# A searched order replaced by another: attention and MoE on one core, with each load tied to an exponential of its own

## The chip, the core and the metric

The kernel runs on one core of a Trainium2 chip. The metric is the device time of one execution in microseconds; the median of three runs of the kernel before is 357.67 us (357.56 to 357.82).

## What is computed

Attention with pooled queries for 8 batches of 8 heads, and a two-branch maximum layer on its output:

```python
B, H, S, D = 8, 8, 1152, 64
q_pool = q.reshape(B, H, S // 2, 2, D).mean(axis=3)          # 576 queries a head
scores = (1.0 / sqrt(D)) * q_pool @ k^T                       # 576 x 1152
attn = softmax(scores);  attn_out = attn @ v                  # 576 x 64
x = attn_out.transpose(0, 2, 1, 3).reshape(B * 576, 512)      # 4608 tokens
h1 = x @ w1;  h2 = x @ w2                                     # 512 x 1024 each
out = maximum(h1, h2) @ w_out                                 # 1024 x 512
```

Inputs and output are float32; the kernel's matmuls take bfloat16.

## The kernel before

The kernel writes every engine's instruction list out of one recorded order. `Plan.op` records an operation with its engine, what it reads and what it writes; `Plan.solve` works out which semaphores each must wait for, and leaves out waits that are already known to be over; `emit` then writes each engine's operations in the recorded order. No engine looks ahead: PE (TensorE), ACT (ScalarE), DVE (VectorE), POOL (GpSimd) and SP, which issues nearly all DMAs, each go through their own list in turn.

The order itself is one long string. Each letter is one step: `S` a group of scores, `E` an exponential, `A` one chunk of attention times V, digits `0` to `3` one unit of a MoE job (each digit is a stream with a job of its own), `l` the next load on SP, `k`, `q`, `v` POOL's casts of K, Q and V, `t` the DMA that transposes K, `x` the DMA that transposes the attention output, `r` one of eight DVE transposes of pooled Q, `e` POOL's copy of a remainder, `o` a store, `4` to `9` copies out of PSUM. Which load is next stands in `LOADS`, which MoE job is next in `MOE` (`w`: product of the weights, `h`: the difference branch, `p`: the output projection), and which PSUM bank a score group or a job takes in `BANKS`.

- **Attention.** Two heads make a head pair; there are 32. K, Q and V of a pair are loaded in float32 (576 KB each) into one of three buffers, and cast by POOL to bfloat16 (`cast_k`, L405; `cast_q`, which also adds neighbouring queries, L435; `cast_v`, L445). K is transposed by a DMA on SP (`ktrans`, L475), Q by DVE (`qtrans_dve`, L485); the first pairs go through PE (L533, L552).
- **Scores and exponentials.** The pairs' scores form one row of 324 groups of 512 columns for both heads; `scores` (L302) fills two PSUM banks with a group, `exps` (L317) has ACT write its exponential to `et`. Where a group crosses into the other half of `et`, ACT does it in two pieces, so there are 336 instructions.
- **Attention times V** (`av_jobs`, L621; remainders L636): nine matmuls make a chunk of 128 queries of one head. V carries a column of ones, which gives the sums; DVE takes reciprocals (L651) and scales (L654).
- **MoE.** maximum(h1, h2) = h2 + relu(h1 − h2), so the kernel keeps `wd` = w1 − w2 (L506) and `w21` = w2·w_out (L593). `h_jobs` (L760) computes relu(x·wd), copied out by DVE or ACT (L771, L775); `p_job` (L803) adds x·w21 and relu·w_out over 24 matmul units per 256 tokens, copied out at L809 or L812 and stored (L829, L835). The last tokens go as `z` jobs (L846).

Scores, MoE matmuls and transposes use half of the PE array's rows at a time in pairs ("64*128" in the profile); attention times V uses all rows ("128*128").

A load waits for its buffer and, from the 40th exponential on, for the exponential two before the one that stands last in the recorded order at the load's place:

```python
def pace():
    g = done[0] - PACE
    return [f"E{g}"] if PACE and g >= PACE_FROM else []
```

Of the kernel before, what the change touches and what calls it, by code (L numbers as in the profile page):

```python
# [116 lines left out]
def bass_funnel_attn__then__act_maxout2_kernel(  # L117
# [78 lines left out]
    with ctx:  # L196
# [762 lines left out]
        for c in (  # L959
            "luFFlulllfyKQklgfbSkKEFlgFKSgESyFFlKEFgQSbESlFkSFEFFKlEySFSgESlqFFEFQlSbEFkSQElbKvSEgSlESceAAEATcESA"  # L960
            "EAhlkSaSEaASclEKAEglSAEcSAElvSaTaEhElTcSAESlAhAEScAElSSAcEAAlAqESa0a00aE0la0ScAE0SldQEaa00bSd0lEXSj0"
            "00ESvTl0h0E00eS4SlEAAkAEAlSa1ad1E1S1SEl1q1S1E1Kl1g1qE1S1SE1lQkrAEbArSdtAErArSE11avlEa1S5AElSdArESSrA"
            "dArEArSAEkAlaAaSEaAdatAESaXadjXEjSjSEXq0jl00jE0S0qr0E0lSr01rE11e41Sl1E1Sk1r10Er005St0ESv00r0ESSr0rvE"
            "lA4AAEASqalSaEAArAErAlSrSEEaAeaAArxAErSSaAEaAklrAAErS1at1ak1E1r0Sr0xE0r0Sr11E1rS1r0E050Sl0E0q0SrS0tE"
            "r01r10Er0eS0r0E0r0Skr0lE0r1S0r0E0rlSv0r1E14S11El1S1oSE1oAAEASAkEAaAlaSAEtAvSa1aE1SxS11ES111E1111ES11"
            "l1ESq5AAEAlSrSoEAroArAESrkSArEAaAalAEAaAaSvaaEtaSSrXEqArAjAEAjSrle00Ea0aS0rSE0lr0vSr0E1r01rlE114S11E"
            "1S1rSEA5AlvAEASr0E0ta0Eva0SrSE00xe00SE4AAkAESSlAEAaAaAEAlSa1aE1Sx000E0Sk11E0lS11E11S50qlE00tS00ESer0"
            "0rSE00rS0rE00r00Er0l0qSrSE0r01l1r0E14S11E1l1SroSE1r1o11roSErAoArAtEkArAAaaAArq1ESaa1E1Sx001r001E1r0S"
            "1rE0l001rS141E1rS1r1ES5AAEvAAroSSrvoESAlAAEvAaAaAlEAaAkaSa000SaEt0a000011114Ee111S111115E1S111Xl5EvS"
            "j00j0ESl0qSE0000SEl4AAAEArSSaEAaArAlqEArS1a1taE11rSESrE1e1xrS1r1EA5AAEASla0kaE0Sr00rSEq0l0r0SEr0ArAl"  # L970
            "E4SAAESr11aE1a1Srx1ESr11r1SEt5qAAAEArSe0aE0a0Slr0SEkr0S0r0E0lrS0r0E0r0Sl0rE0000ES0S0Er0tArAEArArS0aE"
            "0aq0Srx10Er1S14k1E1S11EroS1rSo1E1oAAoEvAAS1vElSAAlEAvAaSa1ESalAaAAEASa1aE1taS1rXvE1rS1j11Ej1eSrl11rE"
            "11qrSS5EAlAAkEAroS0a0oEa0S0rS0ErAAlAEASa0a0E0l0S4x00E0qSE0r00E0trSA4eAEAArS1a1Ea1k1Sr11ESr1lSr1E5AAA"
            "lEArS1a1Ea11Srx00E10S1l1E1S500tE0Sq0rS0Er00r0e0ESr00rSEl0kr00r0E0rS0l0ES00SE0A4AAEAAaAoaAoASaoSqaE11"
            "x11SESkr11t1rE11rE11rE1SrS1E1r11r1SEr11S1E1S11E1A5AEvAASoSvESlAAoAEvAaAaAElAaAa0Sa0a0E0taS00r0000E04"
            "e0Sx000r0E11141vS1x1E11r100500Sr11qE1Sr01lr110E1rS050E0Sl0r0E0SS0l0E0S0r0EArAArEAArlAkaAaArSE0etEa0a"
            "S0r0SE0rxS0rq0EA4AAEASkao1aE11o1SSE11lS11EA5AAElASa1aE1Sx0r00E0rS1rt0E0er0Sr0E1S4111ESl1r0q0E500S0lE"
            "0SrS0r0EA4lAAEAAAaaAASa1aESlk1Sx1r1ES1r11Ert11r11Er1qSSr1E1rArAEvAS1E11klS11El11vS1E1S1lvA5ESAAEAoAa"
            "oSaSESaAtaArAEArq00Ea0aSa00rExSv0r00ErS0xe0r0E0rSSr0kl0E0S00E0Sl00E0S00El0A4AEAAAaoSaSEoArAtArE00Ea0"
            "0aeS00rxE1111r00qS411E1111151S1k1E1r1Sl00500ESr000SrEl0A4AAEArSla1aE1S1S1EAAAEAlSa1aE1tSrS1rq1E1r1x1"  # L980
            "1rESSre11Er11rSk1Elr11S1E11Sl1E1A5AAEASaoSaEAoAAoEAoSa0a0tEq00rSESr0E00rx00k040E0AArvAArSrSvElArArAE"
            "AvaAaAAaAaSaSaE00a001x14E11S11E1x11Sv511E100S1SE0r1t11r0ES0500E0eSr00Er00SrSE0r00r0SEr0S00E0S00E0004"
            "0E00S0E0oS00oSE4AAAEAAaAaAeAAaEAaAAxAaAaAASa0aES0x00SE1000E0S411E1S11E111500S0E00S11E1S11E1S10E50S00"
            "E0S10E0Se10E00S00E0S00E0S00E10S41E11S11EoS11o1E1oSSo1E1AAEAAAaAaAAAaAaAxAAAAAaAaAAaAa1a1a1a11X1j11j1"
            "11111900001111111150000111o080110091o110000008101110191101000018111009101110000080101111191100000001"
            "001111910000000011111111110001000800110000o008001o11o00010181111Z9ZZZZZoZZoZZZZZZmZZZZzzZZZZZZZZZZmZ"
            "ZZZZZZzZzmzz"
        ):
            step(c)
# [52 lines left out]
```

## Time and profile before

| | |
|---|---|
| median of 3 runs | 357.67 us (357.56 to 357.82) |
| span of the profiled execution (no other time of it is given) | 356.4 us |
| PE matmul busy | 346.0 us (97%) |
| PE weight loads busy | 218.5 us (61%) |
| ACT busy | 313.8 us (88%) |
| DVE busy | 230.1 us (65%) |
| POOL busy | 151.4 us (42%) |
| exponentials (L317) | 336 instructions, 302.4 us |
| DMA | 84.55 MB, mean 237 GB/s |
| granted PE clock | 0.999 |

The span runs from the first to the last instruction of one execution. "PE" is matmuls, "PEld" the weight loads, which overlap them; the ends of matmuls are modelled, so a busy PE is not PE at its peak. In rows of waits, the engine and line on the left stood still until the one behind the arrow was done; "issue" means that the profile shows nothing that it waited for.

### The profile page before, as it was taken

What the parts mean: (1) busy time and instruction counts of PE and PEld (TensorE: products, weight loads), DVE (VectorE), ACT (ScalarE), POOL (GpSimd) and SP (SyncE); (2) the same over time, 40 slices, a digit from 0 to 9 for tenths busy, and PEclk for the clock granted to TensorE, in tenths of its full rate; (3) what the DMA queues carried; (4) which work ended last, traced back from release to release, by engine and by line L of the source; (5) the groups of instructions that cost most, each with busy time, mean ns of one, the idle gap of its engine ahead of it and who ended that gap; (6) DMA issues with size and microseconds to landing.
All of it is one profiled execution on the core that took longest, in us unless ns stands there. A gap on an engine that the chain in (4) does not pass through costs nothing.

```text
span 356.4 us, 13757 instructions
## 1 busy us (share of the span) xinstructions
PE 346.0 (97%) x6178; PEld 218.5 (61%) x6178; DVE 230.1 (65%) x472; ACT 313.8 (88%) x354; POOL 151.4 (42%) x136
## 2 busy tenths in 40 slices
PE   7889999999899999999999999999999999999996
PEld 5556665656564675656666576556576757448753
DVE  2587589974966867985887677785586875414001
ACT  5999999999999899999999989989999796992431
POOL 2625997554564264355544455227444621010000
PEclk9999999999999999999999999999999999999999
DMA  8999999999989989998999699998999943012215
GB/s 271 403 397 398 370 255 309 280 289 261 293 252 279 315 196 350 237 301 183 278 320 260 153 230 301 237 314 234 224 299 255 267 68 75 17 32 47 61 31 148
DMA packets 76699, 84.55 MB, mean 237 GB/s; under 512 B 48480, under 2 KB 49760, under 8 KB 76640
## 3 DMA queue, kind: packets, MB, share of 16 engines
q1 hardware_dynamic: 75856, 83.15, 87.5%
q8 instruction: 48, 0.79, 0.9%
q10 hardware_dynamic: 784, 0.52, 0.5%
q14 instruction: 11, 0.09, 0.1%
HBM read 62.91 MB, written 9.44 MB: 203 GB/s over the span
## 4 chain that ended last, share of the span: by engine, by line
PE 87%; ACT 9%; DMA 2%; issue 1%; SPq 0%; DVE 0%
PE ps L803 25%; PE ps L621 20%; PE ps L302 19%; PE ps L760 16%; ACT et L317 9%; PE ps L636 3%; PE ps L593 2%; DMA qraw<-in_q_dram 2%; PE ps L846 1%; PE ps L552 0%; PE ps L533 0%; SPq L346 0%; DVE qp L428 0%; SPq L358 0%; PE ps L730 0%
## 5 line engine op out<-in xcount | busy, mean ns | idle before, releaser
L317 ACT ACTIVATE et<-ps 128x1024 bf16<-128x1024 f32 (+1 forms) x336 | 302.4, 1019 | 14.5 <-PE ps L302 9.7
L302 PE MATMUL ps<-qpT,kT 64*128 64x256 bf16 (+7 forms) x1162 | 117.3, 283 | 2.7 <-issue 1.1
L485 DVE STREAM_TRANSPOSE qpT<-qp 32x288 bf16<-32x288 bf16 x216 | 101.4, 469 | 10.4 <-PE ps L302 6.1
L760 PE MATMUL ps<-xT,wd 64*128 64x512 bf16 (+3 forms) x832 | 81.2, 311 | 0.2
L302 PEld LDWEIGHTS ps<-qpT,kT 64*128 64x128 bf16 x1162 | 48.3, 94 | 49.7 <-ACT et L317 11.3
L803 PE MATMUL ps<-wo,stage 64*128 64x512 bf16 x544 | 76.4, 376 | 0.0
L435 POOL TENSOR_TENSOR qp<-qraw 128x576 bf16<-128x576 f32 x30 | 42.1, 1406 | 61.1 <-DMA qraw<-in_q_dram 57.3
L621 PEld LDWEIGHTS ps<-vE,et 128*128 128x128 bf16 x1728 | 54.9, 97 | 13.9 <-ACT et L317 9.3
L621 PE MATMUL ps<-vE,et 128*128 128x65 bf16 x1728 | 60.7, 193 | 0.7 <-issue 0.3
L771 DVE TENSOR_SCALAR stage<-ps 128x1024 bf16<-128x1024 f32 (+3 forms) x41 | 39.7, 970 | 21.1 <-PE ps L760 20.6
L760 PEld LDWEIGHTS ps<-xT,wd 64*128 64x128 bf16 x832 | 35.6, 94 | 22.2 <-PE ps L760 1.9
L405 POOL TENSOR_SCALAR kbf<-kraw 128x1152 bf16<-128x1152 f32 x31 | 35.7, 1153 | 26.3 <-DMA kraw<-in_k_dram 25.6
L803 PE MATMUL ps<-w,xT 64*128 64x512 bf16 x272 | 40.8, 377 | 0.0
L803 PEld LDWEIGHTS ps<-wo,stage 64*128 64x128 bf16 x544 | 26.4, 94 | 20.5
L445 POOL TENSOR_SCALAR vE<-vraw 128x1152 bf16<-128x1152 f32 x24 | 27.4, 1154 | 19.4 <-PE ps L636 10.8
L809 DVE COPY stage<-ps 128x1024 f32<-128x1024 f32 x14 | 17.1, 1224 | 23.1 <-PE ps L803 23.0
L468 POOL TENSOR_SCALAR stage<-et 128x1152 bf16<-128x1152 bf16 x14 | 16.1, 1152 | 35.5 <-ACT et L317 35.5
L654 DVE TENSOR_TENSOR xnat<-ps,rc 128x256 bf16<-128x256 f32 (+2 forms) x71 | 27.6, 397 | 2.0
L651 DVE RECIPROCAL rc<-ps 128x4 f32<-128x4 f32 (+2 forms) x64 | 11.6, 182 | 25.9 <-PE ps L621 25.5
L621 PEld LDWEIGHTS ps<-stage,et 128*128 128x128 bf16 x576 | 18.1, 97 | 2.7 <-issue 2.6
L621 PE MATMUL ps<-stage,et 128*128 128x65 bf16 x576 | 19.7, 193 | 0.0
L803 PEld LDWEIGHTS ps<-w,xT 64*128 64x128 bf16 x272 | 12.5, 94 | 8.8 <-DVE stage L771 0.2
(55 smaller groups left out, 155.4 us busy)
## 6 DMA issues: line engine op xcount, KB each, us to landing
vraw<-in_v_dram SPq DMA_DIRECT2D x32, 576.0 KB, 6.1
kraw<-in_k_dram SPq DMA_DIRECT2D x31, 576.0 KB, 6.7
qraw<-in_q_dram SPq DMA_DIRECT2D x31, 576.0 KB, 6.3
out_dram<-stage SPq DMA_DIRECT2D x24, 256.0 KB, 4.1
out_dram<-stage SPq DMA_DIRECT2D x21, 128.0 KB, 3.4
xT<-in_moe_w_dram SPq DMA_DIRECT2D x4, 512.0 KB, 12.2
stage<-in_moe_w_out_dram SPq DMA_DIRECT2D x4, 512.0 KB, 14.1
stage<-in_moe_w_dram SPq DMA_DIRECT2D x4, 512.0 KB, 13.2
```

Of the source, the lines that this page charges most:

```text
L302: last = e.matmul(ps[:, h, col:col + hi - lo], kT[i % 3][rows(h), t, :], qpT[i % 3][rows(h), lo:hi], start=True, stop=True)
L317: op("ACT", lambda e: e.activation(et2[:, :, c:c + z - a], ps[:, :, a - g * W:z - g * W], EXP, scale=scale), r=[f"b{m}", f"b{m + 1}"], w=w ...
L405: op("POOL", lambda g: g.tensor_scalar(kbf[s][:, :, :, :].rearrange("p t h d -> p h t d"), kraw[r][:, :, :, :], 1.0, 1.0, ALU.mult, ALU.mu ...
L435: op("POOL", lambda g: g.tensor_tensor(qpf[s][:, :, :], qraw[r][:, :, 0, :], qraw[r][:, :, 1, :], ALU.add), r=[f"qraw{r}"], w=[f"qp{s}.0", ...
L445: return g.tensor_scalar(vE[r][:, :, :, 0:D].rearrange("p t h d -> p h t d"), vraw[s][:, :, :, :], 1.0, 1.0, ALU.mult, ALU.mult)
L485: op("DVE", lambda e: e.transpose(view[dst:dst + 32, :, 32 * pb:32 * pb + 32], qpf[s][src:src + 32, :, 32 * db:32 * db + 32]), r=[f"qp{s}. ...
L621: last = e.matmul(fb[m][:, at * 66:at * 66 + 65], et[:, a:a + P], vE[vs][:, t, half, 0:65], start=(t == 0), stop=(t == NT - 1))
L654: todo.append(evac_op("DVE", lambda e, m, z=z, at=at, num=num, dst=dst: e.tensor_tensor(dst, a(m)[z, at:at + num, 0:D], rc[k][z, at:at + n ...
L760: last = e.matmul(fb[m + k][:, 0:size], wd[z, ct, (f0 + k) * P:(f0 + k + 1) * P], xT[z, ct, n0:n1], start=(turn == 0 and ct == 0), stop=(t ...
L771: return e.tensor_scalar_max(gT[:, f0:f0 + 2, g0:g0 + size], wide[m // 2][:, :, 0:size], 0.0)
L803: last = e.matmul(fb[m + k][:, :], lhs, rhs, start=(turn == 0 and j == 0), stop=(turn == 1 and j == NC_ + NF - 1))
L809: return e.tensor_copy(osb2[:, o:o + 2, :], wide[m // 2][:, :, :])
```

## The change

The order is replaced as a whole: the step string, `BANKS`, the order of `LOADS`, and one place in `MOE` are new tables. ACT copies 11 MoE results and a `z` block out of PSUM where it copied 14 and one; DVE does the others. The MoE tail uses up to four streams where it used two. The rule for loads is replaced too: a table `PACES` gives each load on SP the number of the exponential that it waits for, or −1 for none.

```diff
-    PACE = 2
-    PACE_FROM = 40
...
+    PACES = (
+        -1, -1, -1, -1, -1, -1, -1, -1, -1, -1, -1, -1, -1, -1, -1, -1, -1, -1, -1, -1, -1, -1, -1, -1,
+        -1, -1, -1, -1, -1, -1, -1, 20, -1, 22, 21, -1, 9, -1, -1, 45, 34, 41, -1, -1, 29, 50, 36, 71,
...
     MOE = (
-        "wwhhhhpphhhhpphhhhhhhhpphhhhpphhhhphhhhpphhhhphhhhphhhhpphhhhhhhhhphphh"
+        "wwhhhhpphhhhpphhhhhhhhpphhhhpphhhhphhhhpphhhhphhhhphhhhpphhhhhhhphhhphh"
...
-        def pace():
-            g = done[0] - PACE
-            return [f"E{g}"] if PACE and g >= PACE_FROM else []
-
-        done = [0]
+        def pace(eng="SP"):
+            g = PACES[issued[0] - 1] if eng == "SP" else -1
+            return [f"E{g}"] if g >= 0 else []
+
...
-                after=([f"kraw0.{c}" for c in K0] if s == 0 and hi - lo == NT else []) + pace() + old,
+                after=([f"kraw0.{c}" for c in K0] if s == 0 and hi - lo == NT else []) + pace(eng) + old,
...
-                done[0] = g
```

Of the orders, three places follow. Line numbers are those of each program; from L302 on, a line of the program before stands six or seven higher in the new one (L302 is now L309, L475 is L481, L621 is L627, L760 is L766, L803 is L809).

PE around the first run of 72 attention matmuls (L621, both heads of one pair), before:

```order
L803 MATMUL ps<-wo,stage 128x512 x8
L302 MATMUL ps<-qpT,kT 128x256 x4
L621 MATMUL ps<-vE,et 128x65 x72
L803 MATMUL ps<-wo,stage 128x512 x2
L302 MATMUL ps<-qpT,kT 128x320 x2
L302 MATMUL ps<-qpT,kT 128x192 x2
```

and now:

```order
L809 MATMUL ps<-wo,stage 128x512 x4
L309 MATMUL ps<-qpT,kT 128x256 x4
L809 MATMUL ps<-wo,stage 128x512 x6
L627 MATMUL ps<-vE,et 128x65 x72
L309 MATMUL ps<-qpT,kT 128x320 x2
L309 MATMUL ps<-qpT,kT 128x192 x2
```

Between the same two groups of scores (L302, L309) stand two units more of the output projection (two matmuls each), and they stand ahead of the run.

PE around the longest run, late in the program, before:

```order
L760 MATMUL ps<-xT,wd 128x512 x4
L302 MATMUL ps<-qpT,kT 128x384 x2
L302 MATMUL ps<-qpT,kT 128x128 x2
L621 MATMUL ps<-vE,et 128x65 x144
L302 MATMUL ps<-qpT,kT 128x448 x2
L302 MATMUL ps<-qpT,kT 128x64 x2
L760 MATMUL ps<-xT,wd 128x512 x2
```

and now:

```order
L309 MATMUL ps<-qpT,kT 128x384 x2
L309 MATMUL ps<-qpT,kT 128x128 x2
L766 MATMUL ps<-xT,wd 128x512 x2
L309 MATMUL ps<-qpT,kT 128x448 x2
L309 MATMUL ps<-qpT,kT 128x64 x2
L627 MATMUL ps<-vE,et 128x65 x45
L309 MATMUL ps<-qpT,kT 128x512 x2
L627 MATMUL ps<-vE,et 128x65 x99
L766 MATMUL ps<-xT,wd 128x512 x4
```

Two groups of scores have moved ahead: one in front of the run, and one into it.

SP around the DMAs that transpose K of head pairs 5 and 6 (kT2 from kbf1, kT0 from kbf0; `qraw`, `kraw`, `vraw` are the loads' buffers, and the semaphores are those of the engines waited for), before:

```order
L475 DMA_TRANSPOSE kT2<-kbf1 128x9x128 [waits sem_POOL]
L358 DMA qraw0<-in_q_dram 128x1152
L358 DMA qraw1<-in_q_dram 128x1152 [waits sem_ACT]
L346 DMA kraw1<-in_k_dram 128x2x576 [waits sem_ACT]
L475 DMA_TRANSPOSE kT0<-kbf0 128x9x128 [waits sem_POOL]
```

and now:

```order
L481 DMA_TRANSPOSE kT2<-kbf1 128x9x128 [waits sem_POOL]
L376 DMA vraw2<-in_v_dram 128x2x576
L376 DMA vraw0<-in_v_dram 128x2x576
L376 DMA vraw1<-in_v_dram 128x2x576
L364 DMA qraw1<-in_q_dram 128x1152
L352 DMA kraw2<-in_k_dram 128x2x576
L481 DMA_TRANSPOSE kT0<-kbf0 128x9x128 [waits sem_PE,sem_POOL]
```

Five loads, none with a wait written at it, now stand between the two; before there were three, two of which wait for ACT.

More of the change, by code (lines that the diff above doesn't have):

```diff
@@ L362, in load_q @@
                 w=([f"qraw0.{lo}"] if hi - lo < QU else [f"qraw{s}"]) + name,
-                after=(["qraw0.0", "qraw0.4"] if s == 0 and hi - lo == QU else []) + pace() + old,
+                after=(["qraw0.0", "qraw0.4"] if s == 0 and hi - lo == QU else []) + pace(eng) + old,
                 dma=f"d_qp{lo}" if hi - lo < QU else f"d_q{s}",
@@ L965, in bass_funnel_attn__then__act_maxout2_kernel @@
[L965 to L974, printed above, removed]
@@ new lines, in bass_funnel_attn__then__act_maxout2_kernel @@
+            "AElSdrSlErlXAjdAEAjSaSaEAdaAaAAEXaqSaEjXSj00Ekj0rS0SrE0kt0rS0Er01v411lE1Sl1e1lrE1Slr00vlE0r0tSr10Eq5"
+            "000SSE4AklAAEASvaSaEArAAlrEArSSEreAEArAAaEqaSSaxAaEAAAEt0aSa00rE0SrSxk0Er011r0qE0r1Sr1E141Sl11El1SrS"
+            "1Er11r00E0reS1r1E1rSq1r1E10rS1rk1ESr11r1E1vS500E00S0roESAlAAElAAaSaSErAArqAE0laSa00rxES0rS0Er00l0r0o"
+            "E0r0St0SE000SE4AAAESrSAEAAvAElSaSatAEvaAAaAEAvSaSaEaSrXEjAeAjAEAkSa0a0ESrSk0tr0ESr000qE1l0141oE1So11"
+            "E1lSSl1EA5AAEASa0at0E0Er0SrSE00rx00rSEA4AlAEAlkSrSEArAerAEAaaS0a0Ea00xSSE0000SE40k000E0SrSt0Er0S0r0E"
@@ new lines, in bass_funnel_attn__then__act_maxout2_kernel @@
+            "0re00rSE0r0q000ESS00vEr0Sr00E0q101E41S11E11roSSrE1l1Sr1t1Er1AAEAAoAaAaoAAoSEa1a1lE1r000x0S0000E14S1r"
+            "lAESrlv11r1ESr11l1E1lS5AEAASoSESAoAAElAaAaAEAaAqaSa000a0Ea0000S40k000E1S0001110Evt14111S5XEjS0j0l0Er"
+            "0lSr00Er0S0vSE4AAAeEArSSrEAAaAaqEA0aSa0E0r0klSr0El0ErSx0e0SE4AAlAEAlSat0aE0Sr00rSESr000rE0rAAE4ASAES"
+            "a0a00Er0kSr00ErS0qt0SE4AAAEeAlSa0aE00rS0r0ESr000rE0Sr00Erq0Sr00E0rSSr0E0rS0r0EArArAEAqSa0a0ESr01rk1E"
+            "lSr100Ev14S11E11SroSEArxAvrAEArSlAEAlAAlaSalSEaAxAaAEASta1a1Ea1Sr1SE1oX11joE1eSj1orSE1rl1v1rSl1E1lr1"
```

47 lines of the change are left out of this document (24 added, 23 removed), and 29 rows, old and new, of tables (LOADS, PACES).

## The prediction

> **What bounds the kernel now.** I read the page first, then the busy time by stretches, the waits, the chain, and the timeline at the places where an engine stood still.
>
> ```profile
> span 356.4 us, 13757 instructions
> PE 346.0 (97%) x6178; PEld 218.5 (61%) x6178; DVE 230.1 (65%) x472; ACT 313.8 (88%) x354; POOL 151.4 (42%) x136
> PE 87%; ACT 9%; DMA 2%; issue 1%; SPq 0%; DVE 0%
> 0.00:60.00 60.00, 54.30 (x1032) 33.70 (x1032) 40.14 (x76) 55.10 (x63) 37.88 (x42) 1.00 1.02 345
> 60.00:128.00 68.00, 66.74 (x1200) 41.88 (x1202) 51.78 (x109) 66.15 (x75) 32.93 (x28) 1.00 1.05 278
> 128.00:188.00 60.00, 59.73 (x1110) 38.33 (x1108) 45.58 (x100) 59.44 (x66) 30.62 (x27) 1.00 1.09 271
> 188.00:321.00 133.00, 132.99 (x2293) 82.36 (x2288) 87.27 (x174) 122.80 (x138) 50.00 (x42) 1.00 0.82 197
> 321.00:354.00 33.00, 32.23 (x557) 22.22 (x553) 5.30 (x16) 10.34 (x17) 0.00 (x0) 1.00 0.28 67
> ```
>
> The columns of the stretches are the busy time of PE, PEld, DVE, ACT and POOL, the PE clock, the DMA share and GB/s. Two engines are close to full. Up to 188 us ACT is the fuller one or level with PE (55.10 of 60, 66.15 of 68, 59.44 of 60), so the exponentials set the pace there. From 188 to 321 us PE is busy for 132.99 of 133 us, and ACT stands for 10.2. Behind the last exponential comes a tail of matmuls, 33 us with PE all but full. A new order that does the same work can only win where one of the two stood still.
>
> ```profile
> 9.43 15.70 ACT et L317 x17
> ...
> ACT et L317 <- PE ps L302: 9.7, 15, 2.1
> PEld ps L302 <- ACT et L317: 11.3, 48, 0.5
> PEld ps L621 <- ACT et L317: 9.3, 27, 0.6
> ...
> ACT et L317 <- PE ps L621: 2.9, 3, 1.1
> ```
>
> An exponential in the full stretch takes 15.70/17 = 0.923 us. By the wait rows (total, times, longest) ACT stood 9.7 + 2.9 = 12.6 us for PE. That is all that a better feeding of ACT could give, and most of it lies where PE was busy all the while, so it can't come back whole. PE's waits for ACT are many and short: 11.3/48 = 0.24 us each.
>
> **The change part by part.** The computation is the same, and so, nearly, is how much of it stands ahead of a given exponential. Adding up the order with unit times as the chain has them (an estimate), 46, 78, 111 and 164 us of matmuls stand ahead of exponentials 60, 96, 132 and 192 in both, and 294 and 296 ahead of the last. So the sum is one of stalls, in six terms.
>
> *1. The hole in the issue of instructions.*
>
> ```profile
> 92.70 0.61 PE L302 MATMUL ps<-qpT,kT 64*128 64x128 bf16 x8 [1.12 <-issue]
> 92.70 0.33 PEld L302 LDWEIGHTS ps<-qpT,kT 64*128 64x128 bf16 x7 [1.38 <-issue]
> ...
> 93.13 4.81 ACT L317 ACTIVATE et<-ps 128x1024 bf16<-128x1024 f32 x5 [0.49 <-PE ps L302]
> ...
> q8 instruction: 48, 0.79, 0.9%
> ```
>
> At 92.70 us PE had waited 1.12 us for nothing that the profile shows, and ACT 0.49 us behind it. The row of the instruction queue (48 packets, 0.79 MB) makes a late block of instructions the likeliest cause. Bounds: −1.1 if the hole goes or falls where ACT has scores in stock, 0 if it only moves, +1.1 if there are two. I take −1.1, since one hole in 356 us is rare and most places have cover. The Trainium skill, "Runtime: NRT & Kernel Launch", section "Instruction fetch mechanics", says that crossing a 16 KiB block is mostly hidden. The trace agrees for all but this one place; going by that rule alone, this term is 0 and the sum 1.1 us higher.
>
> *2. Long runs of attention-times-V matmuls.*
>
> ```profile
> 119.36 2.35 PE L621 MATMUL ps<-vE,et 128*128 128x65 bf16 x72
> ...
> 121.75 2.48 ACT L317 ACTIVATE et<-ps 128x512 bf16<-128x512 f32 x3 [1.15 <-PE ps L621]
> ...
> 298.02 4.52 PE L621 MATMUL ps<-vE,et 128*128 128x65 bf16 x144
> 300.40 0.38 ACT L317 ACTIVATE et<-ps 128x256 bf16<-128x256 f32 x1 [0.91 <-PE ps L621]
> 302.91 1.94 ACT L317 ACTIVATE et<-ps 128x1024 bf16<-128x1024 f32 x2 [2.12 <-PE ps L302]
> ```
>
> A run of 72 leaves ACT without scores for 1.15 us, the run of 144 for 0.91 + 2.12. Ahead of the last score the order had seven runs of 72 and that of 144; now it has five of 72, and the long one is cut into 45 and 99. That saves ACT 2 × 1.15 + 45 × 4.52/144 = 3.7 us. Nearly all of it lies where PE is full, and it comes back only where PE later stood for ACT. Bounds −3.7 and 0; I take a quarter, −0.9, since PE's 132.99 of 133 is nearest to the lower end.
>
> *3. The run of 72 at 119 us.* This one stands in a stretch that ACT sets. One unit of the output projection (two matmuls) stood behind it ahead of the next score; now three stand ahead of it.
>
> ```profile
> 338.39 5.40 PE ps L803 x50
> ```
>
> Two units more are 4 × 5.40/50 = 0.4 us of further hole for ACT. Bounds 0 (a score in stock) and +0.4; I take +0.4, as the row at 121.75 shows no stock.
>
> *4. Scores close behind the exponential that frees their bank.* Counting the matmul work between the two in the order, 50 scores had less than one exponential's length before (48 waits in the trace), and 56 have it now. Six more at 0.24 us are +1.4 at most; nothing if PE's work in flight covers them, as the full PE row says it mostly does. I take +0.3. Changes between half-array and full-array matmuls go from 172 to 174 and, by the same kind of gap (0.24 us), cost 0 to +0.5; within the 0.3.
>
> *5. Loads earlier.*
>
> ```profile
> POOL qp L435 <- DMA qraw<-in_q_dram: 57.3, 22, 6.2
> POOL kbf L405 <- DMA kraw<-in_k_dram: 25.6, 15, 3.5
> ...
> DVE qpT L485 <- POOL qp L435: 0.8, 3, 0.3
> ...
> PEld ps L552 <- POOL kbf L405: 0.6, 2, 0.3
> ```
>
> POOL stood 57.3 and 25.6 us for late Q and K. Counted in exponentials, a load could leave 11 ahead of its cast on the mean and 5 at the least; now it is 18 and 6. Most of POOL's wait will go. But no more than 0.8 us of it reached DVE and 0.6 PE. Bounds 0 and −1.4; I take 0, the transposes of Q having stood far ahead of their scores. The new waits themselves cost nothing by the order: SP is served in turn, and of the 73 loads with a gate 45 stand behind a later gate that has been passed already. Only 28 hold the queue, and behind these stand K's transposes, which is the first rival.
>
> *6. The tail.* PE is busy 32.23 of 33 us, nearly the same units follow, and four MoE streams instead of two fill it. 0, at most −0.5 or +0.5.
>
> Sum: −1.1 − 0.9 + 0.4 + 0.3 + 0 + 0 = −1.3 us. The profiled span of 356.4 becomes 355.1. The page gives no other time of that execution; the median of the runs, 357.67, lies 1.3 above the span, and that stays. Forecast: **356.4 us**, faster by 0.4%. About 0.2% (0.7 us) is what a measurement of this kernel can tell from no change.
>
> **The rivals.**
>
> *K arrives late (slower).* K's transposes are DMAs in the same SP queue as the loads.
>
> ```profile
> kraw<-in_k_dram SPq DMA_DIRECT2D x31, 576.0 KB, 6.7
> xT<-in_moe_w_dram SPq DMA_DIRECT2D x4, 512.0 KB, 12.2
> stage<-in_moe_w_out_dram SPq DMA_DIRECT2D x4, 512.0 KB, 14.1
> ...
> L405 POOL TENSOR_SCALAR kbf<-kraw 128x1152 bf16<-128x1152 f32 x31 | 35.7, 1153 | 26.3 <-DMA kraw<-in_k_dram 25.6
> ...
> DMA to landing us min/median/max: 3.2/5.5/7.5
> ```
>
> The last row is of K's transpose. From cast to first score the order left 13 exponentials at the least (12 us); now head pairs 6, 5 and 9 have 8, 9 and 10, or 7.4, 8.3 and 9.2 us. The cast takes 1.15 and the transpose 5.5 in the median: 6.7 us, so 0.7 us are left for pair 6. At 7.5 us it would be 1.2 late, a gain given back. Five loads of 576 KB are queued right ahead of it; if it lands as the weights did in the crowd of the first 45 us (12.2 to 14.1), or halfway there, at 10 us, its scores wait 1.15 + 10 − 7.4 = 3.7 us, in the stretch that ACT sets, with nothing to cover it: 356.4 + 3.7 = **360.1**. It decides from a landing of 6.3 us on. The Trainium skill, "DMA: Bandwidth & Descriptors", section "Two DMAs through the same engine are not ordered", says that within one queue descriptors start in order; the trace's 12 to 14 us for what stood behind other loads agree. Against it: by then the weights have landed, and later loads took 6.7. Chance 0.22.
>
> *Nothing (same).* The hole in issue stays in another place and the ACT holes of term 2 were PE's anyway: −1.3 + 1.1 + 0.9 = +0.7 by the terms as taken, or 0 with terms 3 and 4 covered. 357.7. That the change doesn't do what it says belongs here: 45 of 73 gates don't bite. Chance 0.22.
>
> *PE stands for ACT (slower).* Terms 3 and 4 in full without 1 and 2: +0.4 + 1.4 + 0.5 = 2.3, or **360.0**. The short lead of six more scores is certain by the order; that each costs PE 0.24 us is not, since its row is full. Chance 0.10.
>
> *More comes back.* Term 2 in full and term 1: −1.1 − 3.7 + 0.7 = −4.1, or 353.6. It needs PE to have been held up by ACT inside its full row. Chance 0.08.
>
> **How the numbers follow.** The forecast has the remaining 0.38. Faster by over 0.2% (below 357.0): forecast and more, 0.46. Same: 0.22. Slower: 0.32. The forecast's own range, from the bounds of terms 1 to 4, is 355.0 to 357.0. The whole range leaves out half of the last case and the upper third of the slower ones, and runs from 354.2 to 360.6.
>
> **What would show it.** Right: no issue hole of over 1 us on PE that ACT feels; ACT's waits for PE down from 12.6 to about 9; POOL's wait for Q well under 57; PE's waits for ACT at scores near 50. Wrong: PE's weight loads for scores waiting on kT's DMA at 45 to 65 us or near 93; the last exponential ending later than 322 us with PE idle ahead of it; two holes of issue.

## The result, and the profile after

The new order takes **367.24 us** (median of four runs, 366.71 to 368.29) where the old one took 357.75 beside it (357.56 to 358.45): a ratio of 1.0254 with a 95% interval of 1.0216 to 1.0293. It is slower, and outside the range forecast. The profiled execution took 366.71 us, span 365.0, so 8.6 us more span than before. Ratios, here and below, are of fast runs alone; of all runs one was slow, at 371.15 us, and it counts only in the median of `new_no_gates`.

The head of the page (span, engines, the chain by engine):

```profile
span 365.0 us, 13737 instructions
...
PE 349.9 (96%) x6178; PEld 220.9 (61%) x6178; DVE 232.4 (64%) x475; ACT 313.0 (86%) x351; POOL 150.7 (41%) x136
...
PE 67%; ACT 18%; DMA 8%; SPq 2%; POOL 2%; issue 2%; DVE 1%; POOLq 0%; ACTq 0%
```

PE is busier than before (349.9 for 346.0 us of the same 6178 matmuls; 3.4 us of this is what two stretches of 3.41 us at half clock would add, an estimate from the clock's record), and its share of the chain fell from 87% to 67%: ACT and DMA now stand in it with 18% and 8%. The same stretches as before (PE, PEld, DVE, ACT, POOL, PE clock, DMA share, GB/s):

```profile
0.00:60.00 60.00, 52.45 (x1010) 33.61 (x1012) 37.92 (x74) 53.39 (x61) 36.64 (x41) 0.97 1.01 354
60.00:128.00 68.00, 65.61 (x1118) 41.42 (x1114) 48.24 (x100) 63.40 (x72) 31.59 (x27) 0.97 0.92 235
128.00:188.00 60.00, 58.25 (x1108) 37.28 (x1103) 45.58 (x97) 57.48 (x64) 26.93 (x23) 1.00 0.98 258
188.00:321.00 133.00, 132.82 (x2302) 82.34 (x2298) 91.37 (x184) 121.97 (x136) 54.37 (x46) 1.00 0.92 216
321.00:354.00 33.00, 33.00 (x600) 22.07 (x598) 8.31 (x19) 13.94 (x18) 1.15 (x1) 1.00 0.22 48
```

In the first two stretches ACT lost 1.7 and 2.8 us, PE 1.9 and 1.1, and the granted clock of PE is 0.97 and not 1.00; in the third they lost 2.0 and 1.5. From 188 us on the rows are like the old ones. The waits answer to those quoted before:

```profile
POOL qp L441 <- DMA qraw<-in_q_dram: 29.5, 7, 9.3
POOL vE L451 <- DMA vraw<-in_v_dram: 28.9, 10, 7.3
...
PEld ps L309 <- ACT et L324: 15.2, 51, 1.2
ACT et L324 <- PE ps L309: 15.0, 25, 1.9
POOL kbf L411 <- DMA kT<-kbf: 14.2, 5, 4.6
...
ACT et L324 <- PE ps L627: 4.6, 4, 2.3
```

ACT stands 15.0 + 4.6 = 19.6 us for PE, where it was 12.6. POOL's wait for Q fell from 57.3 to 29.5 us, but it now waits 28.9 for V and 14.2 for K's transpose to have read the buffer that the next cast writes.

To see where the 8.6 us lie, the starts of the 324 groups of exponentials are read from each trace and compared. "12 to 36" is the time from the start of group 12 to that of group 36. From group 12 to 36 the new order takes 25.3 us for 22.8, from 84 to 96 14.1 for 11.8, from 132 to 144 13.1 for 11.1, and from 276 to the end 85.9 for 84.9. These are four places with +2.5, +2.3, +2.0 and +1.0; all the rest together makes 0.8.

**The first place.** The timeline of the new kernel, start and length, idle before it in brackets:

```profile
22.59 0.61 PE L309 MATMUL ps<-qpT,kT 64*128 64x512 bf16 x6 [1.37 <-DVE kT L574]
22.60 0.33 PEld L309 LDWEIGHTS ps<-qpT,kT 64*128 64x128 bf16 x5 [1.22 <-issue]
23.02 3.83 ACT L324 ACTIVATE et<-ps 128x1024 bf16<-128x1024 f32 x5 [0.46 <-PE ps L309]
...
24.10 0.39 PE L309 MATMUL ps<-qpT,kT 64*128 64x128 bf16 x4 [0.90 <-ACT et L324]
...
27.79 2.11 ACT L324 ACTIVATE et<-ps 128x1024 bf16<-128x1024 f32 x2 [0.93 <-PE ps L309]
...
30.71 0.55 PEld L309 LDWEIGHTS ps<-qpT,kT 64*128 64x128 bf16 x11 [1.20 <-issue]
...
31.14 2.85 ACT L324 ACTIVATE et<-ps 128x1024 bf16<-128x1024 f32 x3 [1.24 <-PE ps L309]
```

PE's weight loads start at 22.60 and at 30.71 us after 1.2 us of "issue" each. The first row names DVE's copy to kT instead, but that copy is not what held PE: with the blocks shifted (below) the same six matmuls start at 22.99 us, 0.02 us after that copy begins. The second place lies 255 PE instructions (matmuls and weight loads) behind the first. The DMA view from 28 to 30 us shows what it waited for:

```profile
q8 instruction: 1, 0.02, 3.5%
```

In narrower windows this one packet of instructions runs from 28.4 to 29.5 us; PE goes on 1.2 us after its end. There are 48 such packets, one for every 256 PE instructions. The two stops, and that of the old order at 92.70 us, lie whole multiples of 256 PE instructions apart, to within one. Setting each packet against the instruction at which its block begins, a packet leaves 0 to 5.8 us after PE has entered the block before, takes 0.9 to 2.6, and in neither trace does PE enter a block less than 1.23 us after the packet's end. In the first 60 us of the new trace, where DMA is busy all the time, the start takes 2.9 to 5.8 us; in the tail, behind 323 us, under 1.6. So a block of 256 instructions takes PE no less than some 5 to 8 us in the first stretch, and PE stops where the order is denser than that. The Trainium skill, "Runtime: NRT & Kernel Launch", section "Instruction fetch mechanics", says that the next 16 KiB block is fetched while the present one runs and that a crossing is mostly hidden; the trace agrees for most of the 47 crossings, not for these.

The old trace has the same boundaries. There PE came to the first only at 22.94 us, 1.53 us after the packet's end, without a stop, and at the second scores stood some 5 to 20 instructions ahead of it; now scores stand up to 20 instructions behind both, and ACT runs dry. And behind the first stop comes something else (same columns as the stretches):

```profile
21.00:22.00 1.00, 0.22 (x16) 0.19 (x9) 0.96 (x3) 1.00 (x2) 0.53 (x1) 1.00 1.03 380
22.00:23.00 1.00, 0.41 (x6) 0.22 (x5) 1.00 (x2) 0.56 (x1) 0.00 (x0) 1.00 1.06 392
23.00:24.00 1.00, 0.21 (x3) 0.00 (x0) 1.00 (x2) 0.97 (x2) 0.32 (x1) 1.00 1.07 400
24.00:25.00 1.00, 0.90 (x24) 0.62 (x26) 0.27 (x1) 1.00 (x3) 0.84 (x1) 0.82 1.01 399
25.00:26.00 1.00, 1.00 (x25) 0.78 (x26) 0.00 (x0) 1.00 (x3) 0.00 (x0) 0.50 1.02 392
26.00:27.00 1.00, 1.00 (x27) 0.94 (x27) 0.99 (x2) 0.86 (x1) 0.00 (x0) 0.50 1.05 390
27.00:28.00 1.00, 1.00 (x14) 0.50 (x12) 0.83 (x1) 0.21 (x1) 0.18 (x1) 0.50 1.06 395
```

From 24.6 to 28.0 us PE has half its clock. It counts as 100% busy there, and ACT is down to 0.21 of a microsecond in 27 to 28. The Trainium skill, "TensorE: Matmul & The Clock Gate", Part 1, has the clock halved after an idle window of about 3.4 us; here 3 us with 0.84 us of work sufficed, and the half clock lasts 3.4.

**The second place** is the rival's, near 93 us, with the pair that it named last (9):

```profile
86.94 3.52 SPq L481 DMA_TRANSPOSE kT<-kbf  x1
...
91.89 3.38 POOL L451 TENSOR_SCALAR vE<-vraw 128x1152 bf16<-128x1152 f32 x3 [7.32 <-DMA vraw<-in_v_dram]
...
95.17 0.93 PE L309 MATMUL ps<-qpT,kT 64*128 64x64 bf16 x12 [1.99 <-DMA kT<-kbf]
...
95.60 1.94 ACT L324 ACTIVATE et<-ps 128x1024 bf16<-128x1024 f32 x2 [1.93 <-PE ps L309]
```

SP comes to K's transpose of pair 9 at 86.94 us, behind four loads, two stores and a transpose of outputs, where the old order issued it at 71.94. POOL's cast of that K had ended at 73.2 us (67.0 in the old order), so the transpose waited 13.8 us for SP's turn, where it was 4.9, and took 8.1 us from there to its landing, where it was 3.2. Of the turn, SP stood 4.5 us at the first of the two stores, for the DVE copy that this store writes out. PE stands 1.99 us for K, ACT 1.93, and half clock follows again from 96.3 to 99.7. POOL had stood 7.32 us for a V that was loaded late. **The third place** has two stops of ACT, 0.7 and 0.9 us long (rows of waits: those of 132 to 150 us):

```profile
138.28 1.40 POOL L441 TENSOR_TENSOR qp<-qraw 128x576 bf16<-128x576 f32 x1 [7.90 <-DMA qraw<-in_q_dram]
140.12 0.33 PEld L766 LDWEIGHTS ps<-xT,wd 64*128 64x128 bf16 x6 [1.23 <-issue]
...
ACT et L324 <- PE ps L309: 1.1, 3, 0.7
ACT et L324 <- POOL rem L474: 0.9, 1, 0.9
```

The first comes behind a late block (PE enters it at 140.12 us, 1.40 us after its packet's end), the second behind POOL, whose copy of a remainder stands in its list behind the late casts of Q and V.

### The profile page after: what moved, and what is told of

Read it like the earlier page. It is cut to its first block, busy times and chain, and to the rows that moved or that the text cites. A ratio compares the mean times of both kernels' runs of the same rounds, so it can differ in the third digit from the quotient of the medians.

```text
span 365.0 us, 13737 instructions
## 1 busy us (share of the span) xinstructions
PE 349.9 (96%) x6178; PEld 220.9 (61%) x6178; DVE 232.4 (64%) x475; ACT 313.0 (86%) x351; POOL 150.7 (41%) x136
## 3 DMA queue, kind: packets, MB, share of 16 engines
q1 hardware_dynamic: 75856, 83.15, 85.4%
## 4 chain that ended last, share of the span: by engine, by line
PE 67%; ACT 18%; DMA 8%; SPq 2%; POOL 2%; issue 2%; DVE 1%; POOLq 0%; ACTq 0%
PE ps L809 19%; ACT et L324 18%; PE ps L627 15%; PE ps L309 14%; PE ps L766 14%; DMA kraw<-in_k_dram 3%; DMA vraw<-in_v_dram 3%; DMA kT<-kbf 2%; PE ps L642 2%; PE ps L852 1%; SPq L376 1%; PE ps L558 1%; SPq L835 1%; SPq L364 1%; PE ps L599 0%
## 5 line engine op out<-in xcount | busy, mean ns | idle before, releaser
L324 ACT ACTIVATE et<-ps 128x1024 bf16<-128x1024 f32 (+1 forms) x336 | 303.5, 1020 | 22.8 <-PE ps L309 15.0
L309 PE MATMUL ps<-qpT,kT 64*128 64x256 bf16 (+7 forms) x1162 | 116.0, 284 | 7.2 <-DMA kT<-kbf 2.0
L766 PE MATMUL ps<-xT,wd 64*128 64x512 bf16 (+3 forms) x832 | 82.5, 312 | 0.9 <-issue 0.8
L309 PEld LDWEIGHTS ps<-qpT,kT 64*128 64x128 bf16 x1162 | 48.7, 94 | 53.6 <-ACT et L324 15.2
L809 PE MATMUL ps<-wo,stage 64*128 64x512 bf16 x544 | 76.4, 376 | 0.0
L627 PEld LDWEIGHTS ps<-vE,et 128*128 128x128 bf16 x1728 | 56.2, 98 | 15.6 <-ACT et L324 9.8
L627 PE MATMUL ps<-vE,et 128*128 128x65 bf16 x1728 | 62.2, 194 | 1.8 <-ACT et L324 1.4
L777 DVE TENSOR_SCALAR stage<-ps 128x1024 bf16<-128x1024 f32 (+3 forms) x44 | 41.6, 949 | 33.0 <-PE ps L766 32.8
L441 POOL TENSOR_TENSOR qp<-qraw 128x576 bf16<-128x576 f32 x30 | 42.1, 1405 | 42.0 <-DMA qraw<-in_q_dram 29.5
L766 PEld LDWEIGHTS ps<-xT,wd 64*128 64x128 bf16 x832 | 35.6, 94 | 24.4 <-PE ps L766 1.6
L451 POOL TENSOR_SCALAR vE<-vraw 128x1152 bf16<-128x1152 f32 x24 | 27.5, 1152 | 39.4 <-DMA vraw<-in_v_dram 28.9
L809 PE MATMUL ps<-w,xT 64*128 64x512 bf16 x272 | 40.5, 377 | 0.0
L809 PEld LDWEIGHTS ps<-wo,stage 64*128 64x128 bf16 x544 | 27.1, 94 | 20.5 <-issue 0.2
L657 DVE RECIPROCAL rc<-ps 128x4 f32<-128x4 f32 (+2 forms) x64 | 11.8, 185 | 29.2 <-PE ps L627 28.8
L627 PE MATMUL ps<-stage,et 128*128 128x65 bf16 x576 | 20.0, 193 | 0.1
L627 PEld LDWEIGHTS ps<-stage,et 128*128 128x128 bf16 x576 | 18.2, 97 | 2.6 <-issue 2.3
L474 POOL TENSOR_SCALAR rem<-et 128x1152 bf16<-128x1152 bf16 x9 | 10.4, 1150 | 19.4 <-ACT et L324 19.4
## 6 DMA issues: line engine op xcount, KB each, us to landing
stage<-in_moe_w_out_dram SPq DMA_DIRECT2D x4, 512.0 KB, 14.1
```

The source lines that it names most:

```text
L309: last = e.matmul(ps[:, h, col:col + hi - lo], kT[i % 3][rows(h), t, :], qpT[i % 3][rows(h), lo:hi], start=True, stop=True)
L324: op("ACT", lambda e: e.activation(et2[:, :, c:c + z - a], ps[:, :, a - g * W:z - g * W], EXP, scale=scale), r=[f"b{m}", f"b{m + 1}"], w=w ...
L441: op("POOL", lambda g: g.tensor_tensor(qpf[s][:, :, :], qraw[r][:, :, 0, :], qraw[r][:, :, 1, :], ALU.add), r=[f"qraw{r}"], w=[f"qp{s}.0", ...
L451: return g.tensor_scalar(vE[r][:, :, :, 0:D].rearrange("p t h d -> p h t d"), vraw[s][:, :, :, :], 1.0, 1.0, ALU.mult, ALU.mult)
L474: op("POOL", lambda g: g.tensor_scalar(rems[s][:, :, :, :], src, 1.0, 1.0, ALU.mult, ALU.mult), r=[f"et{i % 2}.{g - first(i)}" for g in ra ...
L627: last = e.matmul(fb[m][:, at * 66:at * 66 + 65], et[:, a:a + P], vE[vs][:, t, half, 0:65], start=(t == 0), stop=(t == NT - 1))
```

## The experiments

Of each run the expectation is quoted, which was written before it ran. Ratios are to the old kernel on the same chip; in these runs its median was 358.45 to 359.11 us. This table has the four places in us, by the one profiled run of each kernel, while the ratio is of all its runs. The rows shown of the two mixtures and of `old_kT9_late` have the new program's line numbers.

| kernel | 12–36 | 84–96 | 132–144 | 276–end | rest | span | ratio [95%] |
|---|---|---|---|---|---|---|---|
| old | 22.8 | 11.8 | 11.1 | 84.9 | 225.8 | 356.4 | 1 |
| old_small_loads | 22.5 | 11.1 | 11.1 | 84.9 | 225.2 | 354.8 | 0.997 [0.996, 0.999] |
| old_no_gates | 23.0 | 11.9 | 11.1 | 85.4 | 225.5 | 356.8 | 0.998 [0.996, 1.001] |
| old_shift_back16 | 22.7 | 13.0 | 11.1 | 84.9 | 225.4 | 357.1 | 1.003 [1.000, 1.006] |
| old_shift24 | 24.0 | 11.4 | 11.1 | 86.5 | 225.1 | 358.1 | 1.004 [1.001, 1.006] |
| old_kT9_late | 22.6 | 14.2 | 11.1 | 84.9 | 225.6 | 358.4 | 1.009 [1.005, 1.013] |
| old_compute_new_feed | 23.7 | 13.6 | 11.5 | 85.1 | 241.5 | 375.4 | 1.042 [1.040, 1.044] |
| new | 25.3 | 14.1 | 13.1 | 85.9 | 226.6 | 365.0 | 1.025 [1.022, 1.029] |
| new_no_gates | 25.9 | 14.1 | 11.8 | 85.8 | 229.6 | 367.3 | 1.024 [1.019, 1.029] |
| new_Q15_K15_ahead | 28.7 | 14.2 | 11.8 | 85.8 | 227.2 | 367.8 | 1.028 [1.024, 1.032] |
| new_shift24 | 23.6 | 14.2 | 13.3 | 86.9 | 229.1 | 367.0 | 1.024 [1.021, 1.028] |
| new_kT9_ahead | 26.5 | 11.7 | 11.8 | 85.9 | 229.8 | 365.7 | 1.020 [1.015, 1.024] |
| new_three_moves | 23.6 | 11.9 | 11.1 | 86.5 | 227.8 | 360.9 | 1.016 [1.012, 1.019] |
| new_small_loads | 26.0 | 11.0 | 11.1 | 85.8 | 226.0 | 359.9 | 1.010 [1.006, 1.013] |
| new_three_and_small | 23.8 | 11.0 | 11.1 | 85.9 | 226.2 | 358.0 | 1.004 [1.002, 1.006] |
| new_compute_old_feed | 24.1 | 11.1 | 11.1 | 86.7 | 242.1 | 375.1 | 1.052 [1.050, 1.053] |

"Rest" carries some luck: the start of group 12 alone varies from 16.7 to 18.6 us between runs.

### Feed and compute exchanged

The lists of SP and POOL (loads, transposes, stores, casts) were taken from one order and those of PE, ACT and DVE from the other, all else alike.

> The new order on PE, ACT and DVE, with the lists of SP and POOL (loads and their gates, transposing DMAs, stores, casts) as before. Theory feed: SP and POOL go through their lists in turn, and in the new lists a late load holds POOL's casts and the transposes of K behind them; then 6 to 9 of the 9.5 us come back: 358 to 361. Rival compute: the new order of matmuls and exponentials is itself slower (more scores close behind their exponential, longer holes of ACT); then it stays at 365 to 367. Rival fetch: late blocks of instructions make it; with the old loads the holes of issue go back to one, 363 to 364.

> The other half of the exchange: PE, ACT and DVE as before, SP and POOL in the new order with the new gates. Theory feed: the loss comes along, 364 to 368, with PE waiting for K or ACT for POOL. Rival compute: 357.5 to 359. Rival fetch: three holes of issue on PE, 360 to 361.

Measured: 377.26 and 373.80 us, ratios 1.052 and 1.042. Both mixtures are worse than either whole, so neither expectation holds, and the loss can't be shared out between feed and compute. In the first, DVE waits for POOL, whose casts come in the other order, and PE behind it:

```profile
88.48 0.47 DVE L491 STREAM_TRANSPOSE qpT<-qp 32x288 bf16<-32x288 bf16 x1 [6.47 <-POOL qp L441]
...
89.53 0.61 PE L309 MATMUL ps<-qpT,kT 64*128 64x64 bf16 x4 [5.97 <-DVE xnat L660]
```

In the second, the same at another place:

```profile
274.59 0.95 DVE L491 STREAM_TRANSPOSE qpT<-qp 32x288 bf16<-32x288 bf16 x2 [8.01 <-POOL qp L441]
...
276.25 1.04 PE L766 MATMUL ps<-xT,wd 64*128 64x256 bf16 x8 [7.60 <-DVE xnat L660]
```

### Small loads

```diff
-                vraw[s][:, :, :, :].rearrange("p h t d -> p h (t d)"),
+                vraw[s][:, :, 0:(NT if i < 3 else 1), :].rearrange("p h t d -> p h (t d)"),
```

and Q and K likewise.

> The changed kernel, but from the fourth head pair on each load of Q, K and V moves a ninth of its bytes; what it leaves out is that data, so its output is not the reference's. Order, waits and number of DMAs are the same. Theory feed (loads land late) and rival fetch (blocks late in the crowd of loads): POOL's waits for loads and the holes of issue go, 354 to 358. Rival compute: 363 to 366.

> The kernel before with the same cut in the loads' bytes, as the control: the same data is left out. Loads were hidden there except for the one hole of issue: 355 to 357.5 by every theory; the difference to the changed kernel with small loads is what the order of PE, ACT and DVE alone costs or gains.

Measured: 361.67 us, ratio 1.010, for the new order; 357.96, ratio 0.997, for the old. Of 9.5 us 5.6 go in the new order, and 1 in the old. The second and third places are gone (11.0 and 11.1 us). The first stays (26.0): weights and the first pairs, which aren't cut, still keep DMA full from 15 to 30 us (366 to 391 GB/s). The cut doesn't tell late loads from late blocks: from 84 to 96 us the DMA share is 0.53 with small loads, so the packets of instructions have less to stand behind as well.

### The blocks of instructions shifted

PE's warming matmuls at the start (L521, L515 before) were made fewer and wider, or more and narrower, in the same time. All blocks then begin elsewhere in the program.

```diff
-    FILL = 28
+    FILL = 16
```

> The new order with 16 wide warming matmuls at the start in place of 28 (same length in time, 24 PE instructions fewer), so that every block of 256 PE instructions ends 24 instructions later in the program: the scores that stood 2 to 20 instructions behind the block boundaries at 22.6 and 30.7 us now stand ahead of them. Theory 'blocks': a block of PE instructions is not there until about 1.25 us after its fetch has landed, and the two early stops cost so much because scores stood right behind them. PE may still stop at those boundaries, but exponential 24 starts at about 29 us instead of 31.1 and the kernel takes 363.7 to 365.5 instead of 367.2. Theory 'crowd': the two stops come from the loads alone and cost the same wherever they fall; exponential 24 stays at 31 us and the time within 0.5 of 367.2.

> The same shift of 24 PE instructions in the old order. Its one felt stop, at 92.7 us, had eight scores 2 to 15 instructions behind the boundary; they now stand ahead of it. Theory 'blocks': 0.5 to 1.1 us less, 356.6 to 357.3, unless scores that were 25 to 40 behind another late boundary (the one at 35.4 us has some 21 to 35 behind) now feel a stop, then no change. Theory 'crowd': the stop at 92.7 us stays, 357.75 within 0.5.

> The old order with 36 narrower warming matmuls (same length in time, 16 PE instructions more): every block ends 16 instructions earlier in the program. The scores that stood 18 to 5 instructions ahead of the boundary at 29 us now fall behind it, as in the new order. Theory 'blocks': a stop of PE of about 1 us or more at 28 to 31 us that ACT feels, and 0.8 to 2 us more: 358.5 to 359.8; the stop at 92.7 us stays, with its scores up to 16 further behind. Theory 'crowd': nothing there, 357.75 within 0.5.

Measured: 368.25, 359.93 and 360.54 us, ratios 1.024, 1.004 and 1.003. At the place itself theory "blocks" holds. In the new order shifted, PE has no stop at the first boundary and only waits for ACT near 24 us, its scores being through:

```profile
22.00:23.00 1.00, 0.90 (x36) 0.50 (x28) 0.90 (x3) 1.00 (x2) 0.00 (x0) 1.00 1.00 375
23.00:24.00 1.00, 0.77 (x6) 0.20 (x6) 1.00 (x2) 1.00 (x2) 0.00 (x0) 1.00 1.09 407
24.00:25.00 1.00, 0.00 (x0) 0.00 (x0) 1.00 (x2) 1.00 (x3) 0.00 (x0) 1.00 1.00 392
25.00:26.00 1.00, 0.76 (x24) 0.51 (x26) 0.98 (x1) 1.00 (x3) 0.88 (x1) 1.00 1.03 396
```

ACT (fourth pair of numbers) is at 1.00 in every row, the clock stays at 1.00, and groups 12 to 24 take 11.1 us (14.3 before the shift). In the three profiles of the new order with the shift, 12 to 36 takes 23.6 to 23.8 us; in the five without it 25.3 to 28.7. But the time hardly moved, so the number expected was wrong: the second boundary still stops PE (the first row is the wait for ACT),

```profile
25.24 0.39 PE L309 MATMUL ps<-qpT,kT 64*128 64x128 bf16 x4 [1.44 <-ACT et L324]
...
32.40 1.23 PE L627 MATMUL ps<-vE,et 128*128 128x65 bf16 x35 [1.24 <-issue]
```

and the rest was 2.5 us longer, 1.7 of it before group 12. In the old order shifted, the stop at 92.7 shrank to 0.27 us, and two others came:

```profile
29.87 0.85 PE L621 MATMUL ps<-vE,et 128*128 128x65 bf16 x23 [1.30 <-issue]
...
93.21 0.23 PE L552 MATMUL ps<-ident,xnat 64*128 64x64 bf16 x4 [0.27 <-issue]
...
284.86 1.12 PE L621 MATMUL ps<-stage,et 128*128 128x65 bf16 x32 [1.46 <-issue]
```

Shifted back, the stop expected at 29 us didn't come (22.7), and the one at 92 us cost more (13.0 for 11.8). This profile is one of that kernel's faster runs (358.82 us, median 360.54), so it need not show all of the ratio. So a shift decides which boundary hurts; where it will be was not foreseen, and the fetch's start varies between runs (for the second boundary of the new order 5.5 to 6.6 us after PE entered the block before).

### K's transpose of pair 9

Moved ahead in the new order, and back in the old one (SP's list, `kt9` the transpose, `O` stores, `l` loads, `x` output's transpose):

```text
new:            O l l l x l O kt9 l     ->  kt9 O l l l x l O l
old, ahead of:  kt9 l l l O O l kt10 x l l  ->  l l l O O l kt9 x l kt10 l
```

Each `t` of the order takes the next pair's transpose, so in the old order pair 10's moved back too: pair 9's left at 79.83 us (71.94 before), behind four loads and two stores, and pair 10's at 84.00 (81.35 before). It was meant to be pair 9's that leaves at about 85.

> The new order with one DMA moved: the transpose of head pair 9's K goes ahead of four loads and two stores in SP's queue (to about 79 us instead of 86.9). Theory 'K late': PE's 2.0 us wait for kT at 95.2 us goes and the kernel gains 1.5 to 2: 365.2 to 365.8. Theory 'blocks': the block behind the same scores is not there before 95.2 us either, so that only 0 to 0.5 comes back: 366.7 to 367.3. POOL's wait of 7.3 us for V at 84.6 us stays in both.

> The old order with one DMA moved back: the transpose of K of head pair 9 stands behind four loads, two stores and two other transposes in SP's queue, and leaves at about 85 us instead of 72. Theory 'stop and clock': K lands at 91 to 93 us, PE stops for it for some 2 us at the first scores of pair 9, and if it does for so long, the granted clock is at 0.50 for about 3.4 us behind it: 2 to 4 us more, ratio 1.006 to 1.011. Theory 'cover': the scores in stock and the other matmuls hide a late K, ratio 1.000 to 1.003.

Measured: 366.38 us, ratio 1.020 (new: 1.025), and 361.66, ratio 1.009. In the new order the transpose leaves at 78 us, the wait for it is gone, and 84 to 96 takes 11.7 us for 14.1, although a block is late at the same scores:

```profile
78.07 2.29 SPq L481 DMA_TRANSPOSE kT<-kbf  x1
...
97.34 0.61 PE L309 MATMUL ps<-qpT,kT 64*128 64x128 bf16 x7 [1.09 <-issue]
```

Theory "K late" is near: a gain of some 2 us, though the intervals of the two ratios overlap. The mean clock agrees, 0.994 or 0.995 in five of six runs where the new order has 0.990 or 0.991 in all: one stretch at half clock less. In the old order the place lost 2.4 us, as much as expected, but in another way: the transpose left earlier than planned, and no row there has PE waiting for K.

```profile
79.83 2.13 SPq L481 DMA_TRANSPOSE kT<-kbf  x1
...
86.31 1.15 POOL L411 TENSOR_SCALAR kbf<-kraw 128x1152 bf16<-128x1152 f32 x1 [10.03 <-DMA kT<-kbf]
...
88.63 0.47 PE L642 MATMUL ps<-stage,et 128*64 128x65 bf16 x18 [1.53 <-POOL stage L451]
...
90.12 1.94 ACT L324 ACTIVATE et<-ps 128x1024 bf16<-128x1024 f32 x2 [1.17 <-PE ps L309]
...
94.61 0.29 PE L558 MATMUL ps<-ident,xnat 64*128 64x64 bf16 x8 [1.81 <-DVE xnat L660]
```

POOL stood 10.03 us, since the cast of pair 11's K writes the buffer that the late transpose still had to read; V's cast stood behind it in POOL's list, PE's remainder waited 1.53 us for that, and ACT 1.17. PE stopped once more, 1.81 us for DVE. The granted clock stayed at 1.00 in this run, but it is the fastest of the seven (360.09 us, median 361.66); five others have a mean clock of 0.994 or 0.995, about one stretch at half clock, which no trace places. So theory "stop and clock" is neither shown nor ruled out, and a DMA late in SP's list hurts through POOL's list as well.

### Q and K of pair 15, and the gates

The two loads go ahead of the stores before them, with no gate; then, in other kernels, all gates are taken away:

```diff
-            return [f"E{g}"] if g >= 0 else []
+            return []
```

```diff
-    PACE = 2
+    PACE = 0
```

> The new order with only the loads of Q and K of pair 15 moved ahead (to about 117 us from 129, without their gates). Theory 'places': POOL's wait of 7.9 us for Q at 130.4 us goes, the copy of the remainder is there for the exponential at 147 us, and exponentials 132 to 144 take about 11.1 us as in the old order and not 13.1: 1 to 2 us gained, ratio 1.020 to 1.023. Theory 'hidden': POOL only waits somewhere else, the block of instructions at 140.1 us sets that place: within 0.5 of the new order, ratio 1.024 to 1.027.

> The new order with no gate at all: every load leaves as soon as its buffer is free and SP comes to it. Theory 'places' and the forecast's step 5: the gates mostly don't bite, within 1 us of the new order, and if anything less, since the late Q and V come earlier: ratio 1.020 to 1.027. Theory 'gates': it is the waits for the exponentials that make the loads late, so that without them 3 us or more come back: ratio under 1.017. If the gates keep the loads from crowding the instruction blocks and the transposes, it is slower: over 1.028.

> The old order without its gates (no load waits for an exponential; its buffer and SP's turn are all that holds it). Theory 'position': in both orders a load's place among SP's other work and its buffer set when it leaves: within 0.3% of the old kernel. Theory 'gates guard': the old gates keep loads out of the way of the instruction blocks and of K's transposes: 1 us or more slower, ratio over 1.003, with longer landings of kT than 5.5 us in the median and more stops of PE for a block. If earlier loads help, ratio under 0.997.

Measured: 368.48, 368.42 and 358.42 us, ratios 1.028, 1.024 and 0.998. With pair 15 ahead the third place took 11.8 us for 13.1, but the kernel gained nothing; in the profiled run the stop at the second block had grown to 2.78 us, with half clock for 6.8 us behind it:

```profile
31.79 1.05 PE L309 MATMUL ps<-qpT,kT 64*128 64x384 bf16 x11 [2.78 <-issue]
```

The five other runs have a mean clock of 0.991, as the new order has, so this stop doesn't explain their time. The third place is 11.8 in the run without gates and in the one with K's transpose moved too, where POOL still waits 7.6 and 7.0 us for the same Q; so that wait alone isn't its cause. Without gates no difference clear of noise came in either order.

### All together

> The new order with three small moves at once: the blocks of PE instructions shifted by 24 (16 wide warming matmuls for 28), the transpose of K of head pair 9 ahead of four loads, and the loads of Q and K of pair 15, which POOL waited for at 130 to 138 us, ahead of the stores before them and without their gates (issued near 117 us instead of 129). Theory 'places': the loss of the new order sits in these three places (exponentials 12 to 24: 3.2, 84 to 96: 2.3, 132 to 144: 2.0 us more than in the old order by the two profiles), each a stop of PE and, at the first two, about 3.4 us at half the granted clock behind it. 5 to 7 us of the 9.5 come back: a ratio to the old kernel of 1.006 to 1.013. Theory 'whole order': the feed and the compute order are fitted to one another everywhere, and a mended place only uncovers the next: ratio 1.017 to 1.025.

> The new order with the three moves (blocks shifted by 24 instructions, K's transpose of pair 9 and the loads of pair 15 ahead), and besides the loads of Q, K and V of head pairs 3 to 31 cut to a ninth of their bytes, so that the output isn't the reference's. Theory 'places': early stop and late loads are the whole loss and add up; the small loads left 12 to 24 with 3.9 us too much, the three moves left 0.6 to 1.4 there and 1.3 at 180 to 192. With both, only what the order itself costs is left (by the two profiles' stages from exponential 192 to the end some 1 us): span 355.5 to 357.5, ratio 0.996 to 1.003. Theory 'compute order': the order of PE itself is longer whatever the loads do: ratio 1.006 to 1.010, as with small loads alone.

Measured: 363.87 us, ratio 1.016, and 359.85, ratio 1.004. The three moves bring back 3.5 of 9.5 us by the ratios, less than theory "places" and more than "whole order" expected: the three places are shorter (23.6, 11.9, 11.1), but 144 to 276 takes 130.6 us where the new order took 129.3 and the old 128.5. Of these 1.3 us, 0.7 lie in 180 to 192, where ACT waits 1.06 us for POOL's copy of a remainder, and 0.7 in 264 to 276, where PE's weight loads wait 0.95 us for DVE. With small loads as well the span is 3.2 us above the old order's with small loads: 1.3 in groups 12 to 36, where the second block is still felt, 1.0 behind group 276, and 1.0 in the rest. The last two, some 2 us in these two profiles, are what is left for the order of the matmuls itself; by the ratios (1.004 and 0.997) the whole difference is 2.3 us, so it may be less. The rest of the 9.5 us goes with the loads' traffic and the late blocks. No kernel with the whole computation beat the old one measurably.

## Why the prediction was wrong

**Term 5 is the step that failed** ("Loads earlier: bounds 0 and −1.4; I take 0"). The gates do cost nothing, as it said and the runs without them show, and POOL's wait for Q fell well below 57. But the leads were counted in exponentials from the gates and buffers, as if SP's turn cost nothing. For pair 9 the turn alone took 13.8 us (4.9 before), against a lead of 9.2 us for cast and transpose together. A long turn doesn't cost by itself: with small loads it was 17.7 us and the landing 3.9, and moved ahead 2.6 and 6.7, both times without a wait of PE for K; it is turn and landing (13.8 + 8.1 us) that came too late together. POOL's casts stood behind late loads in the same way. Cutting the bytes of the loads brought back 5.6 us; the bound allowed no loss. How much of the 5.6 is late K, Q and V, and how much late blocks, no run separates. The row that "hid" POOL's waits (0.8 us for DVE, 0.6 for PE) belonged to the old order, where the casts stood further ahead of their use.

**The first rival had the place and half of the way,** for pair 9 near 93 us, and priced it at 3.7 us; the wait was 1.99, and the place costs 2.3. Landings did become longer (6.1 us in the median and 12.6 at most, before 5.5 and 7.5), but the rival counted cast and landing alone and left out SP's turn. It expected pair 6 first, whose transpose left as soon as its cast was done, in spite of five loads listed ahead, and did not wait; and it took one such place for all.

**Term 1** assumed that the one hole would go. Two felt holes came in the first 31 us instead and a third at 140.12, and the row at 92.70 was called rare although every 256 instructions have such a boundary. Neither this term nor any other counted PE's half clock behind a stop.

**Term 2** gave nothing. The long run was cut, but ACT still stood behind its second part:

```profile
309.26 2.21 ACT L324 ACTIVATE et<-ps 128x256 bf16<-128x256 f32 x3 [2.30 <-PE ps L627]
```

That is 2.30 us, where the two waits before made 3.03; the 85.9 us from group 276 to the end are 1.0 more than before. The bound of no gain, 0, is what came. **Term 3**: groups 120 to 132 take 13.1 us for 12.9, 0.2 of the 0.4. **Term 4**: 51 waits (forecast near 50 as the sign of right), 15.2 us for 11.3; its share in the loss cannot be told from the stops. **Term 6**: the tail behind the last group's start is 34.0 us for 35.5, outside its ±0.5, but the prediction's own count has 2 us more of matmuls ahead of the last exponential, and these are gone from the tail.

All three signs of "wrong" came: PE waits for kT near 95 us, the last exponential ends at 331.98, and there are three holes of issue.

## What to carry over

In an engine's list that is served in turn, look for what stands ahead of a step and what that waits for, not for how early the step may go: pair 9's transpose lost 13.8 us behind four loads, two stores and a transpose, pair 6's none behind five loads. An order that keeps PE dense while DMA is full runs into late instruction blocks; whether that costs depends on what stands in the few instructions behind each boundary, so a search whose costs leave the blocks out can't see this loss. The two orders here, each fitted to its own feed, could not be mixed.
